# Matmuls of zeros in the idle spells of TensorE, added to open sums of values

## The chip, the cores and the metric

One core of one Trainium2 chip. The metric is the time of one execution on the device, in microseconds (us). The kernel before had a median of 1119.32 us in three runs (1116.41 to 1119.86). "PE" is TensorE, "PEld" its weight loads, "DVE" VectorE, "ACT" ScalarE, "POOL" GpSimd. A ratio of two kernels is the mean time of one kernel's fast runs over the mean of the other's fast runs of the same rounds, so it is not quite the ratio of the medians quoted beside it.

## The reference, cut to what matters

Attention in stripes of a 224 x 224 image with 96 channels. Half of the channels attend within horizontal stripes 8 pixels high, half within vertical ones. Each stripe has 1792 tokens of 48 channels. There are 28 + 28 stripes; the kernel works on them in 28 pairs.

```python
qkv = jnp.einsum('bhwc,cd->bhwd', x, wqkv)
...
ah = _softmax(jnp.einsum('bqc,bkc->bqk', qh, kh) * scale, axis=-1)   # [28, 1792, 1792]
oh = jnp.einsum('bqk,bkc->bqc', ah, vh).reshape(B, H, W, C2)
...                                                                  # the same for vertical stripes
return jnp.einsum('bhwc,cd->bhwd', o, wo)
```

## The kernel before: the parts that matter here

The scores are cut into 1372 tiles of 128 x 1024. ScalarE takes the exponential of 1196 of them, and VectorE computes 176 with a polynomial in five steps. A planner written in Python runs while the kernel is built. It simulates the engines with estimated durations, and each time an engine is free by its estimate it picks the next instruction for it. The order of instructions on every engine is what this planner decides, and semaphores keep it safe. PSUM has eight banks: 0 to 3 hold scores for ScalarE, 4 and 5 those for VectorE, 6 and 7 are shared by the sums of values and all small products ("fills"). A "chunk" is the group of up to 512 query tokens whose sum of values is built up in one bank.

A "spell" is a stretch in which TensorE's granted clock is half. A "window" is one step of 3.41 us on the grid on which the clock changes in these traces.

```python
def add(eng, waits, fn, occ=100.0, done=None, mode=None):
    cnt[eng] += 1
    ops[eng].append((waits, fn, True))
    start = max([now[0], tfree[eng]] + [vis(w) for w in waits])
    ...                                  # + SWITCH if the tile form changes
    tfree[eng] = start + occ             # the planner's clock
    if eng == "pe":
        warm_hist.append((start, start + occ))
```

TensorE's warming matmul, used only where a fill bank or VectorE's bank is free:

```python
def keep_warm():
    t = now[0]
    ...
    busy = sum(b - max(a, t - 3000.0) for a, b in warm_hist)
    if tail[0] or 3000.0 - busy < WARM or t - tfree["pe"] < 60.0:       # WARM = 600
        return False
    if pe_next[0] is not None and pe_next[0] - t < 170.0:
        return False
    bi = fill_bank()
    if bank_free[bi] == "busy" or vis(bank_free[bi]) > t:
        if D["cur"] is not None or vis(D["free"]) > t:
            return False
        bi, w = 4, D["free"]
    ...
    add("pe", [w, e_ident, E_W0], <one matmul of 384 columns into bank bi>, 165.0, mode="r128")
    return True
```

The softmax here doesn't subtract the row's maximum and nothing guards it: scores larger than these inputs give would overflow.

## Time and profile before

| | profiled run of before |
|---|---|
| time of that run; span | 1125.22 us; 1123.0 us |
| ScalarE busy; idle inside its run of exponentials | 1100.9 us; 10.9 us |
| TensorE waiting for ScalarE ahead of scores | 71.8 us |
| mean granted TensorE clock | 0.985 |

The prediction shows the lines that carry the reading. A line of a group gives line number, engine, operation, names, shapes and count, then busy us and mean ns of one, then idle us before them and who ended it. Two more views matter later. The first is ScalarE's timeline in the first spell (start, duration, what, idle before it):

```profile
252.07 1.02 ACT L869 ACTIVATE PTA<-ps 128x1024 bf16<-128x1024 f32 x1 [0.20 <-PE ps L179]
253.63 1.02 ACT L869 ACTIVATE PTA<-ps 128x1024 bf16<-128x1024 f32 x1 [0.54 <-PE ps L179]
255.19 1.02 ACT L869 ACTIVATE PTA<-ps 128x1024 bf16<-128x1024 f32 x1 [0.54 <-PE ps L179]
```

An exponential that stands alone takes 1.02 us, while in a dense row one starts every 0.914 us. So a spell costs more than the idle time in brackets: from start to start it is 1.56 us, not 0.914 + 0.54. The second view is the line of the key correction (minimum, median and maximum ns):

```profile
L483 DVE TENSOR_SCALAR KT_sb<-KT_sb,shift x28: 327/329/352, 7.4 to 1047.0; 128x448 bf16<-128x448 bf16 x27, 128x512 bf16<-128x512 bf16 x1
```

All 28 corrections take one third of a microsecond.

### The profile page before, as it was taken

The page shows a single profiled execution, that of the slowest core. Times are in us where ns is not written, and L with a number is a line of the kernel's source. Part 1 is how long each engine was busy: PE and PEld are TensorE (multiplying, and loading weights), DVE is VectorE, ACT ScalarE, POOL GpSimd, SP SyncE. Part 2 cuts the span into 40 slices and gives each one's busy share as a digit, 9 for nine tenths or more (in the row PEclk, how much of TensorE's full clock was granted, in tenths as well). Part 3 has the DMA queues.
Part 4 walks back from the last instruction along what each step waited for, and adds up shares of the span by engine and source line. Part 5 has one row for each costly group of instructions (what it writes and reads, how often), then busy time and mean ns, then how long its engine had stood idle before and what let it go on. Part 6 is the DMA issues. An engine that isn't in the chain of part 4 may idle for free.

```text
span 1123.0 us, 27671 instructions
## 1 busy us (share of the span) xinstructions
PE 1033.3 (92%) x11849; PEld 368.9 (33%) x11849; DVE 1057.7 (94%) x1757; ACT 1100.9 (98%) x1199; POOL 105.2 (9%) x98
## 2 busy tenths in 40 slices
PE   8999999999999999999999999999999999999997
PEld 2333333332333233333333323332333333333332
DVE  7999999998999899999999999998999999999995
ACT  7999999999999999999999999999999999999997
POOL 0000000000000000000002112112202201210232
PEclk9999999999999899999999999998999999999998
DMA  5301101110110110110111122222122222211111
GB/s 99 73 1 35 34 5 32 34 26 10 35 34 6 30 34 8 28 35 14 22 34 32 39 41 42 39 40 44 38 40 43 40 40 41 42 38 22 27 20 31
DMA packets 168994, 37.29 MB, mean 33 GB/s; under 512 B 168872, under 2 KB 168872, under 8 KB 168872
## 3 DMA queue, kind: packets, MB, share of 16 engines
q1 hardware_dynamic: 167256, 35.35, 16.0%
q8 instruction: 92, 1.51, 0.5%
q10 hardware_dynamic: 1616, 0.18, 0.1%
q14 instruction: 30, 0.25, 0.1%
HBM read 0.15 MB, written 9.63 MB: 9 GB/s over the span
## 4 chain that ended last, share of the span: by engine, by line
ACT 95%; PE 3%; DMA 1%; DVE 0%; SPq 0%; issue 0%; POOL 0%
ACT PTA L869 95%; PE ps L830 2%; PE ps L179 1%; DMA xT_sb<-in_x_dram 0%; SPq L186 0%; PE ps L432 0%; DMA out_dram<-out_sb 0%; PE ps L582 0%; DVE out_sb L617 0%; DVE tmp L594 0%; DVE KT_sb L492 0%; DVE V_sb L401 0%; POOL out_sb L617 0%; DVE rc L588 0%; DVE OT_sb L914 0%
## 5 line engine op out<-in xcount | busy, mean ns | idle before, releaser
L869 ACT ACTIVATE PTA<-ps 128x1024 bf16<-128x1024 f32 x1196 | 1098.7, 1284 | 10.9 <-PE ps L179 10.7
L179 PE MATMUL ps<-QT_sb,KT_sb 49*64 49x512 bf16 (+2 forms) x5488 | 487.6, 368 | 78.8 <-ACT PTA L869 71.8
L830 PE MATMUL ps<-PTA,V_sb 128*64 128x512 bf16 (+1 forms) x2740 | 426.2, 369 | 0.9 <-DVE Ph_sb L554 0.8
L175 PEld LDWEIGHTS <-KT_sb 49*64 49x64 bf16 (+1 forms) x5488 | 139.1, 103 | 347.7 <-issue 336.8
L880 DVE TENSOR_SCALAR tt_sb<-ps 128x1024 f16<-128x1024 uint16 x176 | 214.9, 1221 | 33.8 <-PE ps L179 28.6
L887 DVE SCALAR_TENSOR_TENSOR PTD<-ps,tt_sb 128x1024 uint16<-128x1024 f32 x176 | 214.6, 1220 | 2.0
L617 POOL TENSOR_TENSOR out_sb<-tmp,Ph_sb 128x480 bf16<-128x480 f32 (+2 forms) x89 | 103.6, 1174 | 1011.3 <-DVE sq_sb L884 848.9
L830 PEld LDWEIGHTS ps<-PTA,V_sb 128*64 128x64 bf16 x2740 | 121.2, 108 | 196.9 <-issue 152.6
L886 DVE TENSOR_TENSOR tt_sb<-sq_sb,tt_sb 128x1024 f16<-128x1024 f16 x176 | 121.0, 688 | 3.8
L882 DVE TENSOR_TENSOR sq_sb<-tt_sb 128x1024 f16<-128x1024 f16 x176 | 120.2, 683 | 0.6
L432 PE MATMUL ps<-xT_sb,w_sb 128*64 128x448 bf16 (+3 forms) x448 | 85.5, 379 | 0.8 <-DMA xT_sb<-in_x_dram 0.6
L884 DVE TENSOR_SCALAR sq_sb<-sq_sb 128x1024 f16<-128x1024 f16 x176 | 74.2, 421 | 2.6
L830 PE MATMUL ps<-PTD,V_sb 128*64 128x512 bf16 (+1 forms) x396 | 70.6, 371 | 0.3
L914 DVE CAST OT_sb<-ps 128x512 bf16<-128x512 f32 (+5 forms) x118 | 69.2, 591 | 1.2 <-PE ps L830 1.2
L492 DVE TENSOR_TENSOR KT_sb<-ps,shift 128x448 bf16<-128x448 f32 (+2 forms) x84 | 51.7, 616 | 4.2 <-PE ps L432 4.2
L594 DVE TENSOR_TENSOR tmp<-ps,rc 128x480 f32<-128x480 f32 (+2 forms) x92 | 53.2, 578 | 1.0
L694 PE MATMUL ps<-QT_sb,KT_sb 49*64 49x256 bf16 (+1 forms) x784 | 53.4, 268 | 0.0
L554 DVE TENSOR_TENSOR Ph_sb<-ps,rc 128x480 bf16<-128x480 f32 x84 | 51.9, 617 | 0.4
L401 DVE CAST V_sb<-ps 128x480 bf16<-128x480 f32 (+1 forms) x84 | 51.7, 616 | 0.1
L432 PEld LDWEIGHTS ps<-xT_sb,w_sb 128*64 128x64 bf16 (+1 forms) x448 | 24.5, 106 | 63.1 <-issue 20.4
L468 DVE SCALAR_TENSOR_TENSOR QT_sb<-ps,biasq 128x448 bf16<-128x448 f32 (+2 forms) x59 | 36.3, 615 | 0.0
L464 DVE TENSOR_SCALAR QT_sb<-ps,biasq 128x448 bf16<-128x448 f32 x52 | 35.2, 676 | 0.0
(44 smaller groups left out, 297.6 us busy)
## 6 DMA issues: line engine op xcount, KB each, us to landing
out_dram<-out_sb SPq DMA_DIRECT2D x389, 24.0 KB, 1.9
xT_sb<-in_x_dram SPq DMA_TRANSPOSE x332, 2.5
w_sb<-in_wqkv_dram ACTq DMA_DIRECT2D x2, 54.0 KB, 3.0
out_dram<-out_sb ACTq DMA_DIRECT2D x3, 24.0 KB, 2.1
wo_sb<-in_wo_dram SPq DMA_DIRECT2D x4, 9.0 KB
wo_sb<-one_sb SPq DMA_DIRECT2D x4, 0.0 KB
```

Source lines behind the costliest of these rows:

```text
L175: return e.add_instruction(mybir.InstLdweights(tile_size=(64, 64), tile_position=pos, name=nc.get_next_instruction_name(), engine=mybir.En ...
L179: return e.add_instruction(mybir.InstMatmult(start_tensor_calc=True, stop_tensor_calc=True, tile_size=(64, 64), tile_position=pos, ldweigh ...
L432: ins = e.matmul(o, lhsT=wS[0:kr, wblk(P, kind), :], rhs=x_cols(wdw), start=True, stop=True)
L617: return e.tensor_tensor(out_sb[b][:, wdw, k0:k0 + n, :], tmpi[:, 0:n, :], Ph_sb[:, k0:k0 + n, j, :], ALU.add)
L830: ins = e.matmul(bk[64 * wdw:64 * wdw + 64, 0:qs], lhsT=V_sb[b][:, wdw, kt, :], rhs=pt[:, wdw * 512 + i * qs:wdw * 512 + (i + 1) * qs], st ...
L869: e = add("act", [ev, bufA_ev[sl]], lambda e, base=base, sl=sl: e.activation(PTA[sl][:], ps[:, base * 512:(base + 2) * 512], ACTF.Exp, sca ...
L880: return lambda e: e.tensor_scalar(tt_sb[:], dps.bitcast(U16)[:, 0:2048:2], CS / 65536.0, CS * CA3, ALU.mult, ALU.add)
L882: return lambda e: e.tensor_tensor(sq_sb[:], tt_sb[:], tt_sb[:], ALU.mult)
L884: return lambda e: e.tensor_scalar(sq_sb[:], sq_sb[:], CB, None, ALU.add)
L886: return lambda e: e.tensor_tensor(tt_sb[:], sq_sb[:], tt_sb[:], ALU.mult)
L887: return lambda e: e.scalar_tensor_tensor(PTD[sl][:].bitcast(U16), dps, CC, tt_sb[:], ALU.add, ALU.add)
L914: ev = add("dve", [e_pv], lambda e, dst=dst, sp=sp: e.tensor_copy(dst, sp), t_ps(n), t_ps(n) + 150.0)
```

## The change

The intent is to keep TensorE's clock up where no bank is free for a warming matmul. Zeros are added to the sum of values that is open at that moment, which leaves it as it is.

```diff
-        n_warm = [0]
+        n_warm = [0, 0, 0]
...
                 if D["cur"] is not None or vis(D["free"]) > t:
+                    chg = pv_cur[0]
+                    if KWP and chg < NCHT and not pv_first[chg] and pv_left[chg]:
+
+                        n_warm[1] += 1
+                        pb = bank(6 + chg % 2)
+                        qs = min(256, CH_SIZES[chg % NCH])
+
+                        def zeros(e):
+                            for wdw in range(2):
+                                ins = e.matmul(pb[64 * wdw:64 * wdw + 64, 0:qs], lhsT=ident[:, 0:64], rhs=warm[:, 0:qs], start=False, stop=False)
+                            return ins
+                        add("pe", [e_ident, e_warm], zeros, 115.0, mode="r128")
+                        return True
...                                      # left out: branches on KWL, NRES and RDUE, all 0, which do nothing here
                     return False
```

## The prediction

> **What bounds the kernel now.** I read the page's busy shares first, then the chain that ended last, then ScalarE's group, and last a table of the stretches where that chain leaves ScalarE. The page, parts 1, 4 and 5:
>
> ```profile
> PE 1033.3 (92%) x11849; PEld 368.9 (33%) x11849; DVE 1057.7 (94%) x1757; ACT 1100.9 (98%) x1199; POOL 105.2 (9%) x98
> ...
> ACT 95%; PE 3%; DMA 1%; DVE 0%; SPq 0%; issue 0%; POOL 0%
> ...
> L869 ACT ACTIVATE PTA<-ps 128x1024 bf16<-128x1024 f32 x1196 | 1098.7, 1284 | 10.9 <-PE ps L179 10.7
> L179 PE MATMUL ps<-QT_sb,KT_sb 49*64 49x512 bf16 (+2 forms) x5488 | 487.6, 368 | 78.8 <-ACT PTA L869 71.8
> ```
>
> ScalarE's 1196 exponentials take 1098.7 of the 1123.0 us and carry 95% of the chain. Inside their run ScalarE idles 10.9 us in all, nearly always for the scores (L179). So while the number of exponentials stays, nothing done to TensorE can gain more than 10.9 us, 1.0%. TensorE in turn waits 71.8 us for ScalarE: nearly everywhere it is ahead.
>
> PE's 3% of the chain lies in five places. The table of stretches, cut there (columns: stretch, its length, then busy us and count of PE, PEld, DVE, ACT and POOL, the granted TensorE clock, DMA share, GB/s):
>
> ```profile
> 11.60:250.00 238.40, 219.83 (x2630) 79.55 (x2630) 230.06 (x379) 238.40 (x261) 0.00 (x0) 1.00 0.16 33
> 250.00:258.00 8.00, 7.92 (x50) 1.69 (x46) 4.38 (x8) 6.08 (x8) 0.00 (x0) 0.57 0.28 57
> 258.00:369.80 111.80, 103.06 (x1262) 37.92 (x1262) 109.13 (x180) 111.80 (x123) 0.00 (x0) 1.00 0.11 22
> 369.80:376.80 7.00, 6.92 (x40) 1.31 (x36) 3.55 (x7) 4.98 (x7) 0.00 (x0) 0.51 0.30 62
> ...
> 656.40:660.20 3.80, 3.70 (x22) 0.77 (x20) 3.07 (x6) 2.94 (x5) 2.29 (x2) 0.55 0.24 50
> ...
> 775.20:783.60 8.40, 8.40 (x56) 1.95 (x54) 5.55 (x9) 6.57 (x8) 2.29 (x2) 0.59 0.22 44
> ...
> 1100.80:1107.70 6.90, 6.85 (x40) 1.58 (x38) 4.89 (x10) 4.99 (x6) 1.80 (x3) 0.54 0.18 35
> ```
>
> ScalarE is busy for the whole of every stretch at clock 1.00 and starves only where the clock is about half. Length less ACT busy gives the loss of each cold spell: 1.92, 2.02, 0.86, 1.83 and 1.91 us, together 8.5 us, 1.7 a spell. The other 2.3 us or so of the 10.9 are at the start.
>
> Why it turned cold is in the timeline of TensorE ahead of the first spell (start, duration, what, idle before):
>
> ```profile
> 247.34 1.29 PE L179 MATMUL ps<-QT_sb,KT_sb 49*64 49x512 bf16 x12
> 248.56 0.41 PE L543 MATMUL ps<-wo_sb,OT_sb 128*64 128x97 bf16 x10
> 249.17 0.38 PE L179 MATMUL ps<-QT_sb,KT_sb 49*64 49x512 bf16 x4 [0.20 <-ACT PTA L869]
> 250.09 0.38 PE L179 MATMUL ps<-QT_sb,KT_sb 49*64 49x512 bf16 x4 [0.54 <-ACT PTA L869]
> 250.39 1.06 PE L830 MATMUL ps<-PTA,V_sb 128*64 128x512 bf16 x4
> ```
>
> A chunk's sum of values has just ended, and for three microseconds there are scores and a few final products, with no values (L830). No idle spell is over 0.54 us, and yet the clock falls at 250.37.
>
> **What the Trainium skill says.** "TensorE: Matmul & The Clock Gate", Part 1 (The HAM clock gate): the array's clock is halved or full, decided on a free-running window of 3413 ns. The trace agrees: the clock records read only 1.0 and 0.5, spells last 6.83 or 3.41 us, and all drops lie on one grid (250.37 to 369.83 is 119.46 us, 35 windows of 3.413). The same page, "Why this matters for your kernels", asks for no idle gaps over some 3 us; the trace is stricter, as shown. "PSUM — Partial Sum Buffer", The four PSUM rules, rule 2: a matmul that does not open a group adds where the sum was already written. So zeros added to an open sum leave it alone; results should not change. Zeros do count as activity here: until 6.0 us TensorE has run only the 14 start matmuls of zeros, and the clock is full from 4.6 us.
>
> **The limit, read from the trace.** Eight of those start matmuls (512 columns) take 3.38 us at the slow clock, 0.42 each, so I count 0.21 us of streaming for 512 columns at full clock, with tiles that run side by side once. The windows ahead of the five drops then stream 0.41 to 0.46 of their time; of the windows without a drop the lowest stand at 0.45 to 0.46. The limit is thus near 0.455.
>
> **The change part by part.**
> - *Not moved.* By the instruction order, ScalarE, GpSimd and the DMA queues have the same instructions in the same order; VectorE has the same number, 176 tiles of its own included, with neighbours exchanged. The other new settings (NRES, RDUE, KWL) are zero and do nothing. So the 1098.7 us stay.
> - *Removed.* Three of the old warming matmuls (15 become 12).
> - *Added.* 286 matmuls of zeros, 143 pairs of 256 columns, the two of a pair on different halves of the array. By 0.21 us for 512 columns a pair takes 0.107 us, 143 take 15.3 us. They stand where the planner thinks TensorE idle, and TensorE waits 71.8 us for ScalarE anyway, so at full clock I put nothing of this on ScalarE's path. In a cold spell a pair takes 0.21 us and does count; at 143 pairs per 1196 exponentials a spell of seven has about one, so 0.2 us a spell.
> - *What they prevent.* I laid the order of each program on the measured pace (238.40 / 261 = 0.913 us for an exponential, the other matmuls right behind their scores at 0.21 us per 512 columns) and looked at every position of a 3.41 us window. This is an estimate. Before, it finds 14 dips under 0.455, all at the places where the trace has its own; they cover 4.7 windows' length, so 4.7 cold spells are expected in a run, and 5 were seen. In the changed order the five deepest dips (0.35 to 0.37) go, but about ten dips of 0.40 to 0.43 stand, mostly just after a chunk's last values: there the old sum is closed and the new one not begun, so the new branch may not add anything. Around the 270th exponential, four periods hold five sets of scores (one for VectorE), one group of values and three final products: 5 × 0.21 + 0.43 + 0.12 = 1.6 us of 3.65, 0.44. These ten cover 3.2 windows.
> - *Sum.* 4.7 − 3.2 = 1.5 spells fewer, at 1.7 us: 2.6 us gained; the pairs in the three that remain cost 3 × 0.2 = 0.6. I round the net to 2.2 us. From the three timed runs (median 1119.3, mean 1118.5) this gives 1116.3 to 1117.1; I choose **1116.7 us**.
>
> **The rivals.**
> 1. *All spells go.* The planner's own view is a 3 us history, and the zeros do land ahead of several old spells; if the real limit is 0.40 rather than 0.455, no dip is left. Then 4.7 × 1.7 = 8 us go: about 1111. Against it: drops were seen after windows at 0.45, and no value is open where the change would have to act.
> 2. *Nothing gained.* Which dips are hit depends on where the free window starts. The before runs spread over 3.4 us (1116.4 to 1119.9), two spells' worth, so luck is as large as the gain: 1119 to 1120.
> 3. *Zeros delay what ScalarE waits for.* A pair that starts just before scores become possible, or a switch between tile forms, holds the scores 0.1 to 0.2 us. If each of 143 did so on ScalarE's path, 0.15 × 143 = 21 us would be lost, 1140. Against it: ScalarE did not starve once in the warm stretches, where scores are ready a whole exponential ahead. I give it little.
> 4. *VectorE becomes the bound.* It is 94% busy and its exchanged neighbours could hold a bank longer; but its work is the same, and in warm stretches it never starved ScalarE before.
>
> **Range and chances.** 2% are 22 us. A gain of that size is more than the 10.9 us there are: 0.01. A loss of it needs rival 3 in full: 0.02. The rest, 0.97, is within. For the range I take one spell and a half of luck either way (2.5 us) and the span between rivals 1 and 2: 1112.5 to 1120.0.
>
> **What would show it.** The profile after should have 1196 exponentials in about 1098 us, ScalarE's idle time before them 5 to 9 us instead of 10.9, two to four half-clock spells, on a 3.41 us grid and following a chunk's end, 286 new matmuls (their group some 15 to 40 us busy, since listed durations include the pipeline), and full ScalarE in every warm stretch. TensorE's wait for ScalarE should shrink by some 10 us. No half-clock spells at all would mean that I set the limit too high; as many as before, that the dips left over are deeper than the order tells; ScalarE idle at clock 1.00 would mean rival 3.

## More of the kernel before

A "stall" is the time by which the start of an exponential on ScalarE comes later than 0.914 us after the one before it.

The key correction is on VectorE: it reads bf16 from SBUF and writes it back. The final add of an output is on GpSimd, ordered behind a VectorE instruction ("gate") so that it should run beside VectorE work that reads PSUM:

```python
def ev2(e, bk):                          # key correction
    return e.tensor_scalar(KT_sb[b][:, q0:q0 + qs], KT_sb[b][:, q0:q0 + qs], shift[b][:, 0:1], None, ALU.add)
...
if safe(dur) or len(pool_q) > 3:         # the planner's view of VectorE
    pool_q.pop(0)
    fin((s_dve, cnt["dve"] - 1, 0.0))    # the gate; then out_sb = tmp + Ph_sb on GpSimd
```

The profiled run was slower than all three timed runs.

## The result, and the profile after

The changed kernel has a median of 1126.97 us in four runs (1125.53 to 1129.41), the kernel before 1119.59 us (1116.41 to 1119.86, four runs). The ratio of the fast runs is 1.0075, with a 95% interval from 1.0048 to 1.0102. The result is correct, but the kernel is 0.75% slower where a gain of 0.2% was predicted, and the median lies 7 us above the predicted range.

The page of the changed kernel, parts 1, 4 and 5:

```profile
PE 1054.9 (94%) x12132; PEld 376.3 (33%) x12132; DVE 1062.5 (94%) x1757; ACT 1102.0 (98%) x1199; POOL 108.2 (10%) x98
...
ACT 88%; DVE 6%; PE 4%; issue 1%; POOL 1%; DMA 1%; SPq 0%
...
L874 ACT ACTIVATE PTA<-ps 128x1024 bf16<-128x1024 f32 x1196 | 1099.9, 1280 | 13.6 <-PE ps L183 13.3
L183 PE MATMUL ps<-QT_sb,KT_sb 49*64 49x512 bf16 (+3 forms) x5488 | 487.9, 368 | 62.0 <-ACT PTA L874 46.5
...
L1138 PE MATMUL ps<-warm,ident 128*64 128x256 bf16 x286 | 38.7, 283 | 0.0
```

ScalarE's own work is the same to 1.2 us, but it idles 13.6 us instead of 10.9. The 286 zeros are there. TensorE waits 25 us less for ScalarE, so the zeros fill mostly time in which it had waited. The chain now has VectorE in it (6%, before 0%).

This trace has seven spells between the first rise of the clock and the last exponential (at 11.65, 380.29, 499.76, 619.23, 817.20, 936.67 and 1056.13 us), against five before. The one at 11.65 us need not come from the change: traces of both orders below have one that starts at 11 to 14 us, though that of before has none. **No matmul of zeros starts in any of the 3.41 us windows that end in one of the seven** (the nearest pair starts 0.17 us ahead of one).

What happens ahead of the spell at 817.20 us is in three timelines. TensorE:

```profile
814.02 0.40 PE L183 MATMUL ps<-QT_sb,KT_sb 49*64 49x512 bf16 x4
814.92 0.38 PE L183 MATMUL ps<-QT_sb,KT_sb 49*64 49x512 bf16 x4 [0.51 <-ACT PTA L874]
816.05 0.60 PE L183 MATMUL ps<-QT_sb,KT_sb 50*64 50x512 bf16 x8 [0.75 <-DVE PTD L892]
```

VectorE, and GpSimd at the same time:

```profile
813.02 0.69 DVE L891 TENSOR_TENSOR tt_sb<-sq_sb,tt_sb 128x1024 f16<-128x1024 f16 x1
813.63 1.17 DVE L487 TENSOR_SCALAR KT_sb<-KT_sb,shift 128x448 bf16<-128x448 bf16 x1
814.72 0.17 DVE L592 RECIPROCAL rc<-ps 128x4 f32<-128x4 f32 x1
814.81 1.19 DVE L892 SCALAR_TENSOR_TENSOR PTD<-ps,tt_sb 128x1024 uint16<-128x1024 f32 x1
```

```profile
813.18 1.48 POOL L621 TENSOR_TENSOR out_sb<-tmp,Ph_sb 128x480 bf16<-128x480 f32 x1 [3.74 <-DVE shift L484]
```

Read from the bottom. The GpSimd add is released at 813.18 us, when two VectorE instructions that work on SBUF alone (L891 and the key correction L487) are still to finish. The key correction then takes 1.17 us instead of 0.33. VectorE's last polynomial step (L892) ends 0.84 us late, at 816.00. Only then may the next scores for VectorE (50 rows, L183) be written to its bank. TensorE executes in order, so it stands still for 0.75 us, and the scores for ScalarE that are queued behind it are late as well. The same line for all 28 corrections of this trace:

```profile
L487 DVE TENSOR_SCALAR KT_sb<-KT_sb,shift x28: 326/337/1173, 7.5 to 1051.9; 128x448 bf16<-128x448 bf16 x27, 128x512 bf16<-128x512 bf16 x1
```

Five of them take 1.17 us: at 615.8, 696.3, 813.6, 932.8 and 1051.9 us. The page "SBUF — State Buffer" of the Trainium skill, section "SBUF: two separate sides", gives a reason: VectorE and GpSimd share one pair of ports as an exclusive lock. On VectorE's side instructions with two inputs from SBUF or in a two-port mode take it; whoever starts first holds it for its whole instruction, and the other waits. The add takes 1.48 us here and 1.10 us where nothing overlaps it, and the correction loses 0.84 us.

The pitch of ScalarE (start to start, less 0.914 us) at these places shows stalls outside the spells: 0.66 us at 618, 0.21, 0.19 and 0.24 us at 698 to 703, 0.39 at 815, 0.39 at 934, 0.39 and 0.29 at 1053 to 1055, together 2.8 us. The trace of before has no such stall over 0.11 us after the start. Four of these places are also where the windows become thinnest (weighed below), and four of the seven spells (619.23, 817.20, 936.67 and 1056.13) start within 4.3 us after a slow correction began.

### The profile page after: what moved, and what is told of

The parts are those of the page before. It is cut to its first block, busy times and chain, and to the rows that moved or that the text cites. A ratio compares the mean times of both kernels' runs of the same rounds, so it can differ in the third digit from the quotient of the medians.

```text
span 1127.0 us, 28237 instructions
## 1 busy us (share of the span) xinstructions
PE 1054.9 (94%) x12132; PEld 376.3 (33%) x12132; DVE 1062.5 (94%) x1757; ACT 1102.0 (98%) x1199; POOL 108.2 (10%) x98
## 4 chain that ended last, share of the span: by engine, by line
ACT 88%; DVE 6%; PE 4%; issue 1%; POOL 1%; DMA 1%; SPq 0%
ACT PTA L874 88%; PE ps L835 2%; PE ps L183 2%; DVE tt_sb L885 1%; DVE tmp L598 1%; DVE PTD L892 1%; DVE sq_sb L887 1%; POOL out_sb L621 1%; DMA xT_sb<-in_x_dram 0%; DVE sq_sb L889 0%; DVE OT_sb L919 0%; SPq L190 0%; PE ps L436 0%; DVE KT_sb L480 0%; DVE tt_sb L891 0%
## 5 line engine op out<-in xcount | busy, mean ns | idle before, releaser
L874 ACT ACTIVATE PTA<-ps 128x1024 bf16<-128x1024 f32 x1196 | 1099.9, 1280 | 13.6 <-PE ps L183 13.3
L183 PE MATMUL ps<-QT_sb,KT_sb 49*64 49x512 bf16 (+3 forms) x5488 | 487.9, 368 | 62.0 <-ACT PTA L874 46.5
L892 DVE SCALAR_TENSOR_TENSOR PTD<-ps,tt_sb 128x1024 uint16<-128x1024 f32 x176 | 214.2, 1217 | 1.3
L621 POOL TENSOR_TENSOR out_sb<-tmp,Ph_sb 128x480 bf16<-128x480 f32 (+2 forms) x89 | 106.6, 1206 | 1012.4 <-DVE tmp L598 651.5
L891 DVE TENSOR_TENSOR tt_sb<-sq_sb,tt_sb 128x1024 f16<-128x1024 f16 x176 | 121.2, 689 | 3.7
L1138 PE MATMUL ps<-warm,ident 128*64 128x256 bf16 x286 | 38.7, 283 | 0.0
```

The costliest lines, as they stand in the source:

```text
L183: return e.add_instruction(mybir.InstMatmult(start_tensor_calc=True, stop_tensor_calc=True, tile_size=(64, 64), tile_position=pos, ldweigh ...
L621: return e.tensor_tensor(out_sb[b][:, wdw, k0:k0 + n, :], tmpi[:, 0:n, :], Ph_sb[:, k0:k0 + n, j, :], ALU.add)
L874: e = add("act", [ev, bufA_ev[sl]], lambda e, base=base, sl=sl: e.activation(PTA[sl][:], ps[:, base * 512:(base + 2) * 512], ACTF.Exp, sca ...
L891: return lambda e: e.tensor_tensor(tt_sb[:], sq_sb[:], tt_sb[:], ALU.mult)
L892: return lambda e: e.scalar_tensor_tensor(PTD[sl][:].bitcast(U16), dps, CC, tt_sb[:], ALU.add, ALU.add)
```

## The experiments

Twelve kernels ran, each timed in five rounds beside the kernel before. One run (1156.22 us at clock 0.749, the profiled one of the first kernel below) is left out. That leaves thirteen traces. Runs of before on these two chips were more spread than the first ones: 1118 to 1128 us. All differences are below 2%, so each is given with its 95% interval.

How I weigh a window, here and below: over 3.41 us I add up, for each matmul, its streaming time (2.4 columns per ns at full clock, twice the rate at which 512 columns take 0.42 us at half clock in the start of the trace; placed at the end of its record) times the share of the 128 x 128 array that it uses (rows times columns). A score group counts 0.213 us x 4 x 49 x 64 / 16384 = 0.163 us. With the window ending 0.1 us after the clock's record, over the thirteen traces 33 of 4145 windows at full clock ended in a drop, the idle end after the last exponential left out. Sorted by this share, a single limit near 0.366 puts all but 2 windows on their right side. In the trace after, the windows with drops at 380, 500 and 619 us have 0.36 to 0.37, those at 817, 937 and 1056 us about 0.30; the next one without a drop has 0.38. With rows alone as the weight 14 windows are on the wrong side, with columns alone 19, and with streaming time without the share of the array, as the prediction took it, 10 or more.

The same limit holds on the way up. Counted in the same unit of work, a window at half clock is followed by full clock when it holds at least 0.368, with 3 of 60 windows on the wrong side. A spell thus ends when the work of a window is back at the limit, however busy TensorE looks at half clock.

"Expected spells" below is the length of all positions of a window under that limit divided by 3.41 us, from 12 us to the last exponentials: 3.0 in the trace of before, 4.4 in the trace after. These numbers depend on how positions that touch a spell are counted (two other ways gave 2.5 and 3.4 for before, 3.5 and 5.0 for after, 1.9 both times for the order whose collisions are removed below), so only their order and rough differences carry weight.

### Both kernels again

No edit. 

> The kernel before once more, for more traces and for the clock of each run. Theory A (the order costs): 1116 to 1121 us, 1 to 5 half-clock spells, no stall of ScalarE over 0.15 us at clock 1.00 outside the start. Theory B (luck with the phase of the clock's window): some runs reach 1125 us or more, as the profiled run of before did.

Measured: five runs from 1120.38 to 1124.97 us, ratio 1.001 (0.998 to 1.004) as it should be, mean granted clock 0.989.

> The changed kernel once more. Theory A (the new order makes VectorE late near 618, 698, 815, 934 and 1053 us, which starves ScalarE there and empties TensorE's window): 1124 to 1129 us, again with stalls of 0.2 to 0.7 us at these places and one-window spells after 815, 934 and 1053. Theory B (luck): the stalls do not come back at the same places, and some runs are under 1121 us.

Measured: 1123.66 to 1135.09 us, median 1128.6, ratio 1.0071 (1.0032 to 1.0109), mean clock 0.984. The stalls came back at the same exponentials (0.47 us at 615, 0.40 at 811, 0.40 and 0.30 at 930, 0.39 and 0.30 at 1049), again five corrections take 1.17 us, and spells follow at 813.5 and 933.0 us. Expected spells: 4.1. So it is the program and not luck.

Sixteen runs of before and ten of after (four of these from the first session) give the split. A straight line through before's spans against the time spent at half clock (span x 2 x (1 - clock)) rises 0.34 us for each us at half clock. The changed kernel's runs spent 34.2 us at half clock, those of before 22.3. That is 4.0 us of the 6.0 by which the mean spans differ (1125.7 against 1119.7). The other 2.0 us are of the size of the stalls.

### The new order without the zeros

```diff
-            cnt[eng] += 1
-            ops[eng].append((waits, fn, True))
+            if fn is not None:
+                cnt[eng] += 1
+                ops[eng].append((waits, fn, True))
...
-                        add("pe", [e_ident, e_warm], zeros, 115.0, mode="r128")
+                        add("pe", [e_ident, e_warm], None, 115.0, mode="r128")
```

The planner still believes that it placed zeros, so every engine has the changed kernel's order, and no zeros are executed. 

> The changed kernel's instruction order on every engine with the 143 pairs of zeros left out. Theory A (the order costs, the zeros do not): as slow as the changed kernel or slower, 1125 to 1131 us. Theory C (executing the zeros costs): back to 1117 to 1121 us.

Measured: median 1127.64 us, ratio to before 1.0059 (1.0020 to 1.0099), mean clock 0.984, five corrections of up to 1.172 us, stalls at the same places. The mean is 1128.35 us against 1128.70 with zeros. **Executing the zeros makes no difference that these runs resolve (each kernel's six runs spread over 11 to 14 us); their place in the plan is what costs.**

### The zeros in the old order

```diff
-                        add("pe", [e_ident, e_warm], zeros, 115.0, mode="r128")
-                        return True
...                                      # left out: the same test of the recent activity, counting these zeros
+                        cnt["pe"] += 1
+                        ops["pe"].append(([e_ident, e_warm], zeros, True))   # tfree, warm_hist, alarms untouched
+                        z_end[0] = t + sw + 115.0
+                        return False
```

Taking the 107 pairs out again leaves the order of before exactly, on every engine; as this kernel is edited from the changed one, the other new settings do nothing. 

> The order of before on every engine, unchanged, with 107 pairs of zeros slipped into TensorE's stream where its planner saw it idle. Theory A (the order costs, the zeros do not): no slower than before, and by fewer spells faster, 1113 to 1119 us. Theory C (executing the zeros costs): 1123 to 1128 us.

Measured: median 1122.08 us, ratio 1.0004 (0.9975 to 1.0033), mean clock 0.990, the same as before's 0.990. Not slower, as expected, but not faster either. Expected spells from the trace are 2.9, and 2.9 again when the zeros are left out of the count: they do not stand in the thin windows.

### The new order without the collisions

```diff
...                                      # left out: k_fixed is filled where each correction is planned
+        for i, (waits, fn, inc) in enumerate(ops["pool"]):
+            gates = [w[1] for w in waits if w[0] is s_dve]
+            for kc in k_fixed:                   # places of the key corrections in VectorE's order
+                if gates and max(gates) in (kc - 3, kc - 2, kc - 1):
+                    ops["pool"][i] = (list(waits) + [(s_dve, kc, 0.0)], fn, inc)
```

This is the changed kernel, zeros included. Exactly five GpSimd adds meet the condition, and each waits two VectorE instructions longer. 

> The changed kernel, zeros included, but with the five GpSimd adds that overlap a key correction of VectorE (0.33 us alone, 1.17 us in these five) made to wait until that correction is done. Theory A1 (the new order makes these five collide, which delays VectorE's scores, blocks TensorE in its order and empties the window): all corrections take 0.33 us, the stalls of 0.2 to 0.7 us go, the dips at 695, 812, 931 and 1050 us are no deeper than 0.32 of the array, the mean granted clock comes back to 0.989 to 0.991 and the time to within 0.2% of before. Theory A2 (the new order is worse in other ways, the five are only a sign of it): still 0.4 to 0.7% slower than before, clock 0.985.

The same place as above, now on VectorE and on GpSimd:

```profile
807.40 0.69 DVE L893 TENSOR_TENSOR tt_sb<-sq_sb,tt_sb 128x1024 f16<-128x1024 f16 x1
808.00 0.33 DVE L487 TENSOR_SCALAR KT_sb<-KT_sb,shift 128x448 bf16<-128x448 bf16 x1
```

```profile
808.41 1.10 POOL L623 TENSOR_TENSOR out_sb<-tmp,Ph_sb 128x480 bf16<-128x480 f32 x1 [4.54 <-DVE KT_sb L487]
```

And ScalarE's group of that run, to set against the 13.6 us:

```profile
L876 ACT ACTIVATE PTA<-ps 128x1024 bf16<-128x1024 f32 x1196 | 1097.4, 1312 | 4.7 <-PE ps L183 4.6
```

Measured: median 1118.76 us (1117.71 to 1124.88), ratio to before 0.9988 (0.9956 to 1.0020), mean clock 0.992; the longest correction takes 0.353 us. The mean is 1120.07 us, 8.6 us under the changed kernel's 1128.70 on the same chip. Expected spells fall from 4.1 in the run above to 2.0. Five waits, each moved by two VectorE instructions, remove the whole loss. Of the dips that the collisions had deepened, only the one at 693 us is left, at 0.35 of the array; those at 263, 380 and 498 us stay at 0.33 and make most of the 2.0.

### The same without the zeros

The two edits above together. 

> The new order without the zeros and with the five GpSimd adds behind the key corrections. If the zeros never fall where the window is thin (theory A1 with idle zeros): the same as the run with zeros and moved adds, 1117 to 1122 us, clock 0.991 to 0.994, and the same dips near 263, 380 and 498 us, 2.0 windows' length in all. If the zeros were what made that run better than before: 1120 to 1125 us, clock 0.989 or less.

Measured on another chip: median 1120.65 us, ratio to before 0.9984 (0.9940 to 1.0027), mean clock 0.991, expected spells 1.9. Zeros or not makes no difference that these runs resolve. The interval is wide, since one run of 1130.17 us and one of 1114.65 are in it.

### A late VectorE in the old order

```diff
+                if st.get("late"):
+                    cnt["dve"] += 1
+                    ops["dve"].append(([], lambda e: e.memset(zp_sb[0][:, 0:800], 0.0), True))
...
-                             dict(fn=ev2, occ=0.26 * qs + 75.0)]
+                             dict(fn=ev2, occ=0.26 * qs + 75.0, late=P in (16, 18, 21, 24, 27))]
```

> The order of before with a dummy write of about 0.85 us (800 words) put into VectorE's stream ahead of the same five key corrections. Theory A1: 0.3 to 0.7% slower than before, with stalls of some 0.4 us after each of the five places and a lower clock (0.985 to 0.988). If the old order has slack there (theory A2): within 0.15% of before, clock 0.989 to 0.991.

Measured: the dummies took 0.725 us. Each of the five places shows a stall of ScalarE, of 0.45 to 0.49 us, together 2.4 us. The ratio is 1.0027 (0.9987 to 1.0067) and the mean clock 0.987: in the expected direction, but less than the expected 0.3 to 0.7%, and the interval contains 1. The 2.4 us of stalls are 0.21% of the time. Expected spells are 3.1, as before. So a late VectorE by itself makes the stalls. It did not widen the thin windows in this order. My reading is that this takes the new order as well, where the delay falls on the end of a chunk's sum; no run shows this, and I did not find an edit that separates the two further.

### Filling the thin windows themselves

Here the order of before stays and the planner is not asked. After planning, the thinnest stretches of four exponentials are found by the measure above, and the scores of the emptiest exponential in them are computed twice, into the same bank, until every four reach a set share (0.46 of the array).

```diff
+            def fn_twice(e):
+                for r0, c0, wdw, kh in tiles(0):
+                    loaded_matmul(e, bank(base + wdw)[64 * kh:64 * kh + 64, 0:qs], k_ap(kts[0], r0, kh), QT_sb[b][r0:r0 + kk, q0:q0 + qs], (r0, c0))
+                return fn(e)
...                                      # for 67 of the 1196
```

The weights are loaded already, no bank is needed beyond the one that is free at that moment, and the result is unchanged. 

> The order of before, with the score matmuls of 67 exponentials, those in the thinnest stretches of four, computed twice into the same bank (same result). Theory D (the spells come from windows in which under 0.366 of the array streams, and filling just those dips removes them): no half-clock spell between 25 and 1110 us, clock 0.994 to 0.998, 0.4 to 0.7% faster than before, 1114 to 1117 us. If the limit is something else: no change of the clock.

TensorE's timeline at the place that the prediction showed for before:

```profile
247.64 1.51 PE L181 MATMUL ps<-QT_sb,KT_sb 49*64 49x512 bf16 x20
249.08 0.41 PE L545 MATMUL ps<-wo_sb,OT_sb 128*64 128x97 bf16 x10
249.47 0.59 PE L181 MATMUL ps<-QT_sb,KT_sb 49*64 49x512 bf16 x8
250.39 0.38 PE L181 MATMUL ps<-QT_sb,KT_sb 49*64 49x512 bf16 x4 [0.32 <-ACT PTA L877]
```

The count of 20 where there were 12, and of 8 where there were 4, are the repeats. The stretch without start and tail (columns as in the prediction's table):

```profile
11.60:1108.00 1096.40, 1025.63 (x12049) 365.10 (x11773) 1050.88 (x1732) 1094.60 (x1194) 103.52 (x89) 1.00 0.17 33
```

Measured: median 1115.11 us, ratio 0.9958 (0.9924 to 0.9992), no spell between the start and the last exponential, granted clock 0.999 to 1.000 in five of six runs. Four of the six agree within 0.02 us. One took 1125.63 us at clock 0.985, without a trace.

For the next kernel the first of the two passes streams zeros:

```diff
-... k_ap(kts[0], r0, kh), QT_sb[b][r0:r0 + kk, q0:q0 + qs], (r0, c0))
+... k_ap(kts[0], r0, kh), warm[r0:r0 + kk, 0:qs], (r0, c0))
```

> The same as the run with scores computed twice, but the first of the two passes streams zeros against the same weights. Theory Z1 (a matmul of zeros counts as activity): the same clock and time as that run. Theory Z2 (zeros do not count): clock 0.989 to 0.991 and the time of before.

Measured: median 1115.10 us, ratio 0.9954 (0.9925 to 0.9983), mean clock 0.997 in both. Two of the six runs were slower (1118.45 and 1121.42 us, clock 0.994 and 0.992) and have no trace. The traced run has full clock throughout, as with scores:

```profile
11.60:1108.00 1096.40, 1025.54 (x12049) 365.17 (x11773) 1050.87 (x1732) 1094.60 (x1194) 103.56 (x89) 1.00 0.17 33
```

**Zeros do count as activity.** The change failed by where its zeros stood and by what they did to the plan, not by being zeros.

### Fewer repeats, and the start

```diff
-            if low >= 0.46 * 4 * 914.0:      # stop once every four exponentials reach this share
+            if low >= 0.42 * 4 * 914.0:
```

This leaves 20 repeats. 

> The order of before with only the 20 thinnest score groups computed twice, instead of 67. Theory D: the estimate of the order says no window falls under 0.366 (lowest 0.379), so no spell after 25 us, and fewer of the small stalls of 0.1 to 0.25 us that 67 repeats brought: 1113 to 1115 us in most runs. If the margin is too small: one or two spells again, 1116 to 1119 us.

Measured: median 1120.00 us (1116.83 to 1123.95), ratio 0.9972 (0.9942 to 1.0002). This missed the expected 1113 to 1115 us. The trace has no spell after 38 us, but one from 11.1 to 38.4 us:

```profile
11.10:38.40 27.30, 26.96 (x153) 5.58 (x151) 18.07 (x32) 19.52 (x20) 0.00 (x0) 0.50 0.37 72
```

It costs 9.0 us. TensorE is busy for 26.96 of the 27.30 us, and yet seven of the eight windows hold only 0.27 to 0.37 of the array at full clock, at or under the limit; the last has 0.38, and the clock rises.

```diff
+        for _ in range(4):
+            add("pe", [e_warm], lambda e: e.matmul(bank(7)[:, :], lhsT=warm[:, 0:128], rhs=warm[:, :], start=True, stop=True), 216.0)
         for f in [pf0["K"][1], pf0["V"][0], ...]:
```

Four zero matmuls in a bank that is free, while TensorE waits for the first transposed input. 

> As the run with 20 groups twice, with four more matmuls of zeros into a free bank while TensorE waits for the first transposed input at 8.6 to 9.6 us. If the slow runs of 1118 to 1126 us among the ones with repeats come from a spell at 11 to 25 us: no such run is left, spread under 2 us, 1113 to 1115 us. If the zeros delay the start: 0.3 to 0.9 us more than the run without them.

Measured: median 1115.36 us, ratio 0.9942 (0.9912 to 0.9971), five runs within 1114.77 to 1115.73, one of 1121.23 at clock 0.993 without a trace. So one slow run was left, against what I expected.

The same on the new order without zeros and collisions, with a set share of 0.43 and so 25 repeats: 

> The new order without zeros and collisions, with 25 score groups twice and the four start matmuls. If nothing but spells and collisions set the two orders apart: the same time as the old order with 20 groups twice, within 0.15%, no spell after 25 us.

```profile
L885 ACT ACTIVATE PTA<-ps 128x1024 bf16<-128x1024 f32 x1196 | 1096.5, 1291 | 2.6 <-PE ps L186 2.6
```

Measured: six runs from 1115.09 to 1116.01 us, median 1115.57, ratio to before 0.9935 (0.9909 to 0.9961), clock 0.999. ScalarE idles 2.6 us inside its run. The two orders are now equal within 0.07% of their means. This is the version to keep: 0.65% faster than before, where the changed kernel was 0.7% slower, and with a spread of under 1 us. That it is steadier than the kernel above rests on one slow run in six there and is not shown.

## Why the prediction was wrong, by its steps

- **What bounds the kernel: right.** ScalarE stays the bound, its 1196 exponentials take the same time, and the only losses are spells and stalls.
- **"VectorE has the same number ... with neighbours exchanged": this step failed.** It was booked as moving nothing. The exchange let five GpSimd adds run into five key corrections, 0.33 to 1.17 us each. Rival 4 named the right engine ("exchanged neighbours could hold a bank longer") and was dismissed for having the same work. Moving the five adds gave back 8.6 us.
- **"ten dips ... cover 3.2 windows": failed for the same reason.** The estimate laid each order on an even pace and could not know of the collisions. The traces show 4.1 to 4.4 expected spells with them, and 2.0 without. My estimate done again with the share of the array gives 3.1 for before and 1.9 for the changed order, so it fits the kernel whose VectorE is on time.
- **"the zeros do land ahead of several old spells": wrong.** No zeros start in a window that ends in a spell. Leaving them out of the count of a collision-free trace changes nothing (2.0 both ways). The fewer dips belong to the order, by chance, and not to the zeros. That the new branch may not act once a sum is closed was seen and is right.
- **The limit at 0.455 of streaming time: half right.** The measure that sorts the windows is weighted with the used array, and its limit is near 0.366.
- **"1.7 us a spell": too small.** It counted idle time alone. From start to start, a spell of two windows costs 2.7 us and one of a single window 1.2 to 1.7 us, since an exponential that stands alone takes 1.02 us and not 0.914. The bound of 10.9 us on any gain has the same flaw: start to start, the five spells of before alone cost 12.2 us.
- **A slip in the sum.** 2.6 less 0.6 is 2.0 us, which was "rounded" to 2.2. It changes nothing here.
- **The zeros cost nothing at full clock: right** (rival 3 falls). With and without them the new order has 1128.70 and 1128.35 us. The sign set for rival 3, ScalarE idle at clock 1.00, did come (2.8 us of stalls), but these stay when the zeros are left out and go when the adds move.
- **The range was too narrow.** It allowed 2.5 us of luck either way, from three runs. Later fast runs of before alone went from 1118 to 1128 us.

Putting the sum together with measured terms: 1.3 expected spells more (4.3 against 3.0) at 1.4 to 2.7 us are 2 to 3.5 us, and the stalls are 2.8 us, together 5 to 6 us. On the same chip the means of the two kernels differ by 6.8 us, in the first session by 8.4 us. The interval for the same chip is as wide as 4 to 12 us, so this agreement is a check of the size only. Whether before was lucky in the first session or the chip was another one is not on record.

## What to carry to other kernels

When a planner decides the order, an instruction that costs nothing still moves everything behind it; compare the orders on all engines, and look for pairs of VectorE and GpSimd instructions that now overlap. Put filler in after planning, at places found by the measured limit, and prefer repeating a matmul into its own bank, which needs no free bank. Before predicting a gain of a few microseconds from one trace, get the spread of the kernel before.

## What the Trainium skill lacked or had wrong

- "TensorE: Matmul & The Clock Gate" advises against idle gaps over some 3 us and tells of a kernel whose clock swings with short idle spells, but gives no limit of activity. Here the clock halved 33 times in thirteen traces, and the longest idle spell of TensorE in a window that ended in a drop was 0.96 us. The limit is near 0.366 of the array, weighted by rows and columns in use, over one window of 3.41 us, and the same 0.368 of work per window for the way back up.
- The same page does not say whether matmuls of zeros count for the clock gate. They do: scores computed twice and zeros ahead of scores gave the same mean clock (0.997) and the same median time (1115.1 us).
- The same page calls the window free-running, which the grid of 3.413 us in the traces agrees with. It does not say that spells can follow each other in step. The plan repeats every 128 exponentials (117.4 us at 0.917 us each), a spell adds 1 to 3 us, and 35 windows are 119.46 us. The spells at 817.20, 936.67 and 1056.13 us are exactly that far apart. That this keeps them in step is argued and not shown.
- The same page speaks of some 3.4 us of activity until the clock rises. No page tells of a fall right after that without an idle gap. In eight of the thirteen traces it rose at 4.3 to 7.0 us, fell at 11 to 14 us with no idle spell over 0.96 us and stayed at half for 6.8 to 27.3 us, at a cost of about 2 to 9 us.
- "SBUF — State Buffer" agrees with this case on the lock between VectorE and GpSimd. The case adds its size for a correction of 128 x 448 bf16: 0.33 us alone, 1.17 us behind an add.
